# Removing the engine block of a decode kernel and issuing its first loads ahead of the opening barrier

## The chip, the cores and the metric

The kernel runs on one core of one Trainium2 chip. The metric is the measured time of one execution in microseconds (us). The profile of an execution also gives a *span*: from the first to the last instruction record of the program. The two are not the same, the difference between them called the *gap* here (measured time minus span).

## The reference

One decode step of a transformer layer with one token: layernorm, attention over a cache of 32 heads x 4096 positions x 128, and a gated MLP.

```python
x = A_x                                              # [1, 1, 640], bf16
h  = x + attention(layernorm(x), k_cache, v_cache, wq, wo)
h2 = h + (gelu(layernorm(h) @ w_gate) * (layernorm(h) @ w_up)) @ w_down
# k_cache, v_cache: [1, 32, 4096, 128]; wq: [640, 4096]; wo: [4096, 640]; D = 640, Df = 1728
```

The K and V caches are 33.6 MB each, the weights 17 MB: 84.3 MB are read once from HBM for one token.

## The kernel before

The kernel records, per engine, a list of operations with their dependencies, and then emits the lists inside an engine block. A semaphore wait goes in front of each operation that needs one.

```python
    def emit(self, block):
        ...                                   # one semaphore per DMA, one per engine
        for eng in self.ENGINES:
            getattr(block, eng)(lambda e, eng=eng: self._run(e, eng))
```

The first loads are x (issued by ACT) and wq, K group 0, K group 1, V group 0 (issued by SP). Everything later is issued by SP, too, each time a slot of a ring of three comes free.

```python
    d_x = P.dma("scalar", x_row[:, :], A_x[0, :, :])
    ...
    d_wq = [P.dma("sync", arena[:, :], A_wq[:, :].rearrange("(p c) n -> p (c n)", c=5))]
    ...
    issue(NSLOT)                              # K0, K1, V0 into the three slots
```

The end: four copies bring the output row out of PSUM, two on DVE and two on ACT; SP stores it and waits for the store to land.

```python
    os = [V(lambda e, q=q: e.tensor_copy(out_row[0:1, 160 * q:160 * q + 160], ps_d[32 * q:32 * q + 1, 0:160]), dn)
          for q in range(2)]
    os += [A(lambda e, q=q: e.copy(out_row[0:1, 160 * q:160 * q + 160], ps_d[32 * q:32 * q + 1, 0:160]), dn)
           for q in range(2, 4)]
    d_out = P.dma("sync", out[0, :, :], out_row[:, :], *os)
    P.op("sync", None, d_out)                 # SP waits for the store

    with nc.Block() as block:
        P.emit(block)
```

Two things are not in this source. The program object puts an *opening barrier* in front of everything: every engine drains and reports, POOL first fills four constant tiles, and then releases the others. And the block puts a branch in front of each engine's list, a branch after it, and a *closing barrier* of the same kind, with POOL again as the engine that gathers and releases.

The softmax here doesn't subtract the row's maximum and nothing guards it: scores larger than these inputs give would overflow.

## Time and profile before

| | before |
|---|---|
| time, three runs | 205.62, 205.82, 205.85 us |
| span of the profiled run | 204.0 us (its time: 205.85 us) |
| moved by DMA | 84.47 MB, 414 GB/s on average |
| busy share PE / DVE / ACT / POOL | 59% / 49% / 30% / 2% |

From the profile's page of the kernel before: the span in 40 slices of 5.1 us, with the busy share of the 16 DMA engines in tenths (9 is 90% or more) and the rate, then the totals, then the chain that ended last, by engine.

```profile
DMA  7999999999999999999999999999999999999991
GB/s 249 434 442 411 411 488 430 418 411 442 430 430 424 418 427 463 424 419 418 443 450 424 421 424 438 443 430 418 424 434 450 389 440 435 413 409 425 415 393 55
DMA packets 4319, 84.47 MB, mean 414 GB/s; under 512 B 466, under 2 KB 724, under 8 KB 1492
...
DMA 64%; PE 14%; DVE 14%; SPq 4%; issue 3%; DVEq 0%
```

The kernel is a stream of loads with a short head and a short tail. Only the first and last slice are not full. The stretch from 17 to 175 us moves 431 GB/s. The Trainium skill (DMA: Bandwidth & Descriptors, § Specifications) gives a fabric ceiling of 435 GB/s for a core's 16 engines, and this trace agrees with it. (Slices of the page that read higher, such as 488, don't contradict it: the page counts a packet's bytes whole in the slice in which the packet starts. With the bytes spread over each packet's time, no slice of this trace exceeds 434 GB/s.)

The head, from the timeline of the kernel before (start and duration in us, then engine, line, operation, out<-in, count; SPq is SP's queue of DMA issues):

```profile
0.80 0.38 SPq L51 DMA_DIRECT2D arena<-in_A_wq_dram  x1
1.24 0.89 SPq L51 DMA_DIRECT2D slot<-in_A_k_cache_dram  x2
...
2.11 0.35 PE L212 MATMUL bank<-one_bf,x_row 1*128 1x1 bf16 x5 [2.11 <-DMA x_row<-in_A_x_dram]
...
16.35 4.05 PE L238 MATMUL bank<-arena,xlnB 128*32 128x512 bf16 x40 [11.27 <-DMA arena<-in_A_wq_dram]
```

SP issues wq 0.80 us into the span; PE, which needs wq for q, sits idle for 11.27 us until it has landed. What SP did in the first 0.80 us is in its list of waits (who waited for what: us in total, times, longest), kernel before. Of its lines only three matter here:

```profile
SPq L441 <- DMA out_dram<-out_row: 0.8, 1, 0.8
SPq L456 <- PEq L456: 0.7, 1, 0.7
SPq L441 <- PEq L441: 0.2, 1, 0.2
```

L456 is the opening barrier (0.7 us) and L441 the end of the block: the wait for the store, and the closing barrier. (The view names PE as the one that ended the waits at the barriers; by the records further down it is POOL that releases.) The tail, from the timeline of the kernel before:

```profile
201.83 0.60 ACT L436 CAST out_row<-bank 1x160 bf16<-1x160 f32 x2 [5.75 <-PE bank L426]
201.83 0.66 DVE L434 CAST out_row<-bank 1x160 bf16<-1x160 f32 x2 [2.70 <-PE bank L426]
202.52 0.32 SPq L51 DMA_DIRECT2D out_dram<-out_row  x1
```

The timeline leaves out semaphore, branch and drain instructions. The trace has them; these are its last records of the kernel before (start us, duration us, engine, operation):

```
203.668 0.033 SP   COMPARE_BRANCH    waits for the output's semaphore
203.827 0.007 SP   DRAIN             reports to the closing barrier
203.860 0.017 POOL EVENT_SEMAPHORE   all have reported
203.938 0.017 POOL EVENT_SEMAPHORE   releases them
203.980 0.017 SP   EVENT_SEMAPHORE   released (then ACT, DVE)
203.991 0.051 PE   EVENT_SEMAPHORE   released: the last record, span 204.042
```

### The profile page before, as it was taken

How to read it: one execution, taken by the hardware profiler on the slowest of the kernel's cores; microseconds unless marked ns; L12 is line 12 of the kernel's file. 1: busy time of each engine (PE TensorE's matmuls, PEld its weight loads, DVE VectorE, ACT ScalarE, POOL GpSimd, SP SyncE). 2: the span in 40 equal slices, each digit the busy share in tenths (PEclk: the TensorE clock that was granted, in tenths of full speed). 3: DMA queues.
4: the chain of work that ended last, by engine and by line, in shares of the span. 5: the costliest groups of instructions: out<-in, count | busy, mean ns of one | idle time of the engine just before them, and what ended most of it. 6: DMA issues, size and time to landing. Idle time of an engine off the chain costs nothing.

```text
span 204.0 us, 2507 instructions
## 1 busy us (share of the span) xinstructions
PE 121.1 (59%) x1009; PEld 58.9 (29%) x1009; DVE 100.9 (49%) x104; ACT 61.1 (30%) x273; POOL 4.1 (2%) x12
## 2 busy tenths in 40 slices
PE   1007049567667808690977297637834787467494
PEld 1003013122222503250324032312411244267482
DVE  3100187799279327924791677287608760101221
ACT  2100103626706610670156035503630363100101
POOL 8000000000000000000000000000000000000000
PEclk9999757978969975998599859988995899965555
DMA  7999999999999999999999999999999999999991
GB/s 249 434 442 411 411 488 430 418 411 442 430 430 424 418 427 463 424 419 418 443 450 424 421 424 438 443 430 418 424 434 450 389 440 435 413 409 425 415 393 55
DMA packets 4319, 84.47 MB, mean 414 GB/s; under 512 B 466, under 2 KB 724, under 8 KB 1492
## 3 DMA queue, kind: packets, MB, share of 16 engines
q1 hardware_dynamic: 4306, 84.32, 97.0%
q8 instruction: 8, 0.13, 0.3%
q14 instruction: 3, 0.02, 0.0%
q10 hardware_dynamic: 2, 0.00, 0.0%
HBM read 84.31 MB, written 0.00 MB: 413 GB/s over the span
## 4 chain that ended last, share of the span: by engine, by line
DMA 64%; PE 14%; DVE 14%; SPq 4%; issue 3%; DVEq 0%
DMA slot<-in_A_k_cache_dram 43%; DVE prod L252 12%; DMA slot<-in_A_v_cache_dram 11%; DMA slot<-in_B_w_down_dram 10%; PE bank L260 10%; SPq L51 4%; PE bank L289 3%; DVE sc L267 2%; PE bank L298 1%; PE bank L426 0%; DVEq L441 0%; DVE out_row L434 0%; PE bank L309 0%; DVE RT L308 0%
## 5 line engine op out<-in xcount | busy, mean ns | idle before, releaser
L260 PE MATMUL bank<-prod,id_b 128*128 128x512 bf16 x256 | 75.8, 457 | 53.6 <-DVE prod L252 53.5
L252 DVE TENSOR_TENSOR prod<-slot,qb 128x4096 bf16<-128x4096 bf16 x32 | 72.4, 2284 | 31.6 <-DMA slot<-in_A_k_cache_dram 31.6
L271 ACT ACTIVATE p_bd<-sc,zero_t 32x32 bf16<-32x32 f32 x128 | 46.4, 363 | 89.0 <-DVE sc L267 87.8
L260 PEld LDWEIGHTS bank<-prod,id_b 128*128 128x128 bf16 x256 | 27.1, 114 | 102.5 <-DVE prod L252 66.1
L267 DVE TENSOR_REDUCE sc<-bank 128x32 f32<-128x512 f32 x32 | 22.0, 688 | 21.5 <-PE bank L260 21.4
L271 ACT ACTIVATION_READ_ACCUMULATOR p_bd<-sc,zero_t 32x1 f32 x128 | 23.5, 184 | 0.0
L289 PE MATMUL bank<-slot,p_bd 128*16 128x512 bf16 x256 | 17.2, 379 | 0.6 <-DMA slot<-in_A_v_cache_dram 0.6
L289 PEld LDWEIGHTS bank<-slot,p_bd 128*16 128x16 bf16 x256 | 9.4, 89 | 4.8 <-DMA slot<-in_A_v_cache_dram 1.1
L238 PE MATMUL bank<-arena,xlnB 128*32 128x512 bf16 x40 | 4.1, 586 | 11.3 <-DMA arena<-in_A_wq_dram 11.3
L298 PE MATMUL bank<-po_sb,hs 128*16 128x128 f32 x64 | 8.4, 274 | 1.1 <-ACT po_sb L293 1.1
L327 PE MATMUL bank<-aP,arena 128*128 128x1 bf16 x160 | 6.7, 178 | 3.8 <-DMA arena<-in_A_wo_dram 3.8
L396 PE MATMUL bank<-hlnT,slot 128*128 128x1 bf16 (+1 forms) x140 | 6.7, 176 | 3.2 <-DMA slot<-in_B_w_gate_dram 3.2
L327 PEld LDWEIGHTS bank<-aP,arena 128*128 128x128 bf16 x160 | 6.6, 131 | 4.0 <-DMA arena<-in_A_wo_dram 2.6
L396 PEld LDWEIGHTS bank<-hlnT,slot 128*128 128x128 bf16 (+1 forms) x140 | 6.3, 118 | 4.1 <-issue 3.8
L242 DVE CAST qb<-bank 128x512 bf16<-128x512 f32 x1 | 0.7, 692 | 13.8 <-PE bank L238 13.8
L293 ACT COPY po_sb<-bank 128x512 f32<-128x512 f32 x8 | 4.7, 586 | 7.6 <-PE bank L289 7.6
L298 PEld LDWEIGHTS bank<-po_sb,hs 128*16 128x16 f32 x64 | 5.5, 96 | 4.5 <-issue 2.1
L223 ACT ACTIVATE ln<-ln,eps_t 128x1 f32<-128x1 f32 x2 | 0.6, 294 | 17.0 <-DVE ln L221 17.0
L238 PEld LDWEIGHTS bank<-arena,xlnB 128*32 128x32 bf16 x40 | 1.6, 141 | 13.3 <-issue 13.3
L383 DVE TENSOR_TENSOR hT<-xx,bank 128x5 f32<-128x5 f32 x1 | 0.2, 161 | 10.3 <-PE bank L327 10.3
L243 ACT CAST qb<-bank 128x512 bf16<-128x512 f32 x1 | 0.6, 586 | 14.3 <-PE bank L238 14.3
L313 DVE TENSOR_SCALAR aT<-bank,rz 16x128 bf16<-16x128 f32 x2 | 0.7, 339 | 6.0 <-PE bank L298 6.0
(59 smaller groups left out, 24.6 us busy)
## 6 DMA issues: line engine op xcount, KB each, us to landing
slot<-in_A_k_cache_dram SPq DMA_DIRECT2D x8, 4096.0 KB, 22.3
slot<-in_A_v_cache_dram SPq DMA_DIRECT2D x7, 4096.0 KB, 17.4
arena<-in_A_wq_dram SPq DMA_DIRECT2D x1, 5120.0 KB, 15.4
slot<-in_A_v_cache_dram SPq DMA_DIRECT2D x2, 2048.0 KB, 20.9
arena<-in_A_wo_dram SPq DMA_DIRECT2D x1, 2560.0 KB, 28.7
slot<-in_B_w_gate_dram SPq DMA_DIRECT2D x1, 2160.0 KB, 15.4
arena<-in_A_wo_dram SPq DMA_DIRECT2D x1, 1920.0 KB, 32.8
slot<-in_B_w_up_dram SPq DMA_DIRECT2D x1, 1296.0 KB, 18.0
```

Of the source, the lines that this page charges most:

```text
L51: ev = self.op(eng, lambda e: e.dma_start(out, in_), *deps, dma=True)
L238: i = e.matmul(ps_q[hf][32 * j:32 * j + 32, :], xlnB[:, c, :], wq_j[:, c, j, 4 * hf:4 * hf + 4, :], start=(c == 0), stop=(c == 4))
L242: qa = V(lambda e: e.tensor_copy(qb[:, 0:4, :].rearrange("p g d -> p (g d)"), ps_q[0][:, :]), qd)
L252: m = V(lambda e: e.tensor_tensor(out=prod[:, s % 4, :, :], in0=kt[:, 32 * u:32 * u + 32, :], in1=qb[:, G, :].unsqueeze(1).to_broadcast([1 ...
L260: i = e.matmul(ps_f[s % 2][:, :], id_b[:, :], prod[:, s % 4, :, 16 * b:16 * b + 16], start=(b == 0), stop=(b == 7))
L267: reds[s] = V(lambda e: e.reduce_sum(sc[:, s % 4, :], ps_f[s % 2][:, :].rearrange("p (g d) -> p g d", d=16), axis=AX.X), folds[s], exps.ge ...
L271: x = A(lambda e, j=j: e.activation(p_bd[32 * j:32 * j + 32, G % 2, 32 * (s % 4):32 * (s % 4) + 32, j], sc[32 * j:32 * j + 32, s % 4, :], ...
L289: i = e.matmul(po[a:a + 16, :], p_bd[:, G % 2, 4 * b:4 * b + 4, :].rearrange("p g j -> p (g j)"), vt[:, 4 * b:4 * b + 4, :], start=(b < 4) ...
L293: evs[G] = A(lambda e: e.copy(po_sb[:, G % 2, :], po[:, :]), pvs[G], hds.get(G - 2))
L298: i = e.matmul(ps_a[0:16, 128 * (G // 4):128 * (G // 4) + 128], hs[:, r, 12 - 4 * g:28 - 4 * g], po_sb[:, G % 2, 128 * r:128 * r + 128], s ...
L327: r = e.matmul(ps_p[:, c:c + 1], wo_sb[:, t, i, c::5], aP[:, t, i:i + 1], start=(t == 0 and c == 0 and i == 0), stop=(t == 1 and i == 15), ...
L396: i = e.matmul(ps[0 if m < 13 else 64:128, m:m + 1], ws, hlnT[:, c:c + 1], start=(c == 0 and m == 0), stop=(c == 4), skip_group_check=True)
```

## The change

The intent: start the stream earlier by the length of the opening barrier, and drop the block's branches and closing barrier. The loads of x, wq and K0 depend on nothing, so they may be put in front of each engine's drain. The rest of each list follows the barrier in one straight program. The final wait of SP stays.

```diff
-    def emit(self, block):
+    def emit(self, early):
 ...
+        insts = self.nc.cur_bb.bb.instructions
+        for eng, n in early.items():
+            at = next(k for k, i in enumerate(insts) if type(i).__name__ == "InstDrain" and i.engine == getattr(self.nc, eng).engine)
+            old = len(insts)
+            self._run(getattr(self.nc, eng), eng, self.lists[eng][:n])
+            new = insts[old:]
+            del insts[old:]
+            insts[at:at] = new
         for eng in self.ENGINES:
-            getattr(block, eng)(lambda e, eng=eng: self._run(e, eng))
+            self._run(getattr(self.nc, eng), eng, self.lists[eng][early.get(eng, 0):])
 ...
-    with nc.Block() as block:
-        P.emit(block)
+    P.emit({"sync": 2, "scalar": 1})
```

More of the change, by code (lines that the diff above doesn't have):

```diff
@@ L69, in emit, with _run @@
                     ev.sem, ev.count = sem, n
+        insts = self.nc.cur_bb.bb.instructions
[6 more added lines that the diff above has]
+            insts[at:at] = new
         for eng in self.ENGINES:
-            getattr(block, eng)(lambda e, eng=eng: self._run(e, eng))
-    def _run(self, e, eng):
+            self._run(getattr(self.nc, eng), eng, self.lists[eng][early.get(eng, 0):])
+    def _run(self, e, eng, ops):
         seen = {}
-        for fn, deps, ev in self.lists[eng]:
+        for fn, deps, ev in ops:
             need = {}
```

## The prediction

> **What bounds the kernel now.** HBM traffic. The page's DMA line shows 84.47 MB at a mean of 414 GB/s in a span of 204.0 us, and a busy share of 9 tenths in every slice but the first (7) and last (1). Counting the trace's packets, all 16 DMA engines are in use without a gap from 1.81 us, where wq's first packet starts, to about 200 us; the last weight packet ends at 200.81. The compute engines are far below (page: PE 59%, DVE 49%, ACT 30%). The chain of waits is 64% DMA. So the time is a head, a saturated stream of 199 us, and a tail (down matmuls, output store, closing barrier).
>
> **What the change does.** No arithmetic, byte, transfer size or order within an engine changes. Each engine loses two branches, all lose the closing barrier, and three DMA issues (x on ACT, wq and K group 0 on SP) move ahead of the opening barrier.
>
> 1. Head (timeline): SP reaches the opening barrier at 0.00 us, is released at 0.72, after POOL's four constant memsets, branches, and issues wq at 0.80 (0.38 us), K0 at 1.24 (0.42), K1 at 1.71. The first packet starts 1.01 us after the issue. Issued at 0.00, it starts at about 1.0: **-0.80 us**, all on the critical path, because the stream behind it never starves. The barrier now waits for SP's two issues and opens at about 1.0 us, so the other engines' setup starts 0.2 to 0.3 us later. That has slack: layernorm ends at 6.7 us and PE waits until 16.35 for wq (11.3 us idle). K1 is issued at about 1.1, with 9 MB still queued.
>
> 2. Branch: the 0.07 us from SP's release to the wq issue includes it, inside the 0.80. The Trainium skill (Runtime: NRT & Kernel Launch, § Instruction fetch mechanics) says that a taken branch outside the fetched pages stalls for a fetch; this trace shows no such stall here. Eight instruction pages of 16 KB (about 1 us each on one DMA engine) are fetched along the way and remain: 0.
>
> 3. Tail: the output's packets end at 203.33 us, SP's wait record is at 203.67, then a branch, a drain at 203.83, and the barrier releases the last engine by 204.04. Without them the program ends with SP's wait, at about 203.70: **-0.34 us**. The same page (§ The ~15µs preamble/postamble breakdown) says the runtime has its own barrier after the kernel, so this one is redundant; no record here shows that. The 1.8 us between span and measured time (205.85) I take as fixed.
>
> Sum: -1.14 us, 0.6%.
>
> **Predicted time: 204.7 us, 204.2 to 205.4 in 8 of 10.** Faster by over 2%: 0.01; within 2%: 0.98; slower by over 2%: 0.01.
>
> **What would show it.** SP's wq issue is the span's first record and wq's first packet starts about 1.0 us into it; wq matmuls start at about 15.5 us; all later landings are about 0.8 us earlier; bytes and busy times unchanged; the last record is SP's wait, about 0.35 us after the output's packet; span about 202.9 us. Wrong if the first packet is not earlier, or if the head's gain shrinks along the stream.
>
> **What would make it wrong.** The measured time may start at something that the early issues don't precede, or end at the runtime's barrier, which absorbs the tail's 0.34: then 204.9 to 205.5. SP's drain might wait for its transfers: the barrier would open some 20 us late and everything slip; improbable. The throttle's half-speed windows (granted clock 0.5 in the tail) may shift against the down matmuls, +-0.2 us.

## The result, and the profile after

| | before | after |
|---|---|---|
| time, median of six runs | 205.62 us (205.38 to 205.85) | 204.24 us (203.40 to 204.52) |
| ratio | | 0.9925, 95% interval 0.9905 to 0.9945 |
| span of the profiled run | 204.04 us | 202.90 us |
| its time | 205.85 us | 204.16 us |
| its gap | 1.8 us | 1.3 us |

Ratios are the mean time of one kernel's fast runs over that of the other's fast runs of the same rounds, so they are not quite the ratio of the medians quoted. The ratio times 205.62 us is 204.08 us.

The change saved 1.4 to 1.7 us, about 0.75%, so the two kernels are the same within 2%, as forecast. The span of this pair fell by the predicted 1.14 us; that it fits to the hundredth is luck, since the spans of the six runs of the changed kernel run from 202.1 to 203.3 us. But the time of the profiled run fell by 1.69 us. The rest lies outside the span, where the profile shows nothing.

The page of the changed kernel, the same parts as of before:

```profile
DMA  9999999999999999999999999999999999999992
GB/s 356 412 422 452 420 413 426 446 455 428 368 426 439 426 423 452 420 428 439 426 439 433 430 426 415 452 439 426 420 430 420 417 436 426 426 407 434 411 401 87
DMA packets 4319, 84.47 MB, mean 416 GB/s; under 512 B 466, under 2 KB 724, under 8 KB 1492
...
DMA 65%; PE 15%; DVE 15%; issue 3%; SPq 2%
```

The same packets and bytes; of the busy shares only those of the first and the last slice changed, and the first slice went from 249 to 356 GB/s. The head, from the timeline of the changed kernel:

```profile
0.00 0.39 SPq L51 DMA_DIRECT2D arena<-in_A_wq_dram  x1
...
0.44 1.15 SPq L51 DMA_DIRECT2D slot<-in_A_k_cache_dram  x2
...
5.40 0.35 PE L221 MATMUL bank<-one_bf,x_row 1*128 1x1 bf16 x5 [5.40 <-DMA x_row<-in_A_x_dram]
...
15.28 4.46 PE L247 MATMUL bank<-arena,xlnB 128*32 128x512 bf16 x40 [8.47 <-DMA arena<-in_A_wq_dram]
```

SP now issues wq as the first record of the span. In the packets of the trace, the first one starts at 1.004 us (before: 1.813) and the last weight packet ends at 200.11 us (before: 200.81). The x row came 3.3 us later than before in this trace (5.40 against 2.11 us), its packet starting at 3.45 us. That is not a property of the change: in the repeat of the same kernel (after_same, below) the packet starts at 1.005 us and PE takes x at 1.53 us, earlier than before. Why it was late here, no run shows. PE still waits 8.47 us for wq afterwards, so it costs nothing.

The waits of SP in the changed kernel; L464 is the opening barrier, L93 the waits of the program:

```profile
SPq L93 <- DMA out_dram<-out_row: 0.8, 1, 0.8
SPq L464 <- PEq L464: 0.2, 1, 0.2
```

SP's wait at the opening barrier went from 0.7 to 0.2 us, and the one at a closing barrier is gone. The tail in the timeline of the changed kernel:

```profile
201.05 0.60 ACT L445 CAST out_row<-bank 1x160 bf16<-1x160 f32 x2 [5.76 <-PE bank L435]
201.05 0.66 DVE L443 CAST out_row<-bank 1x160 bf16<-1x160 f32 x2 [2.73 <-PE bank L435]
201.73 0.31 SPq L51 DMA_DIRECT2D out_dram<-out_row  x1
```

and the trace's last record:

```
202.884 0.017 SP   EVENT_SEMAPHORE   waits for the output's semaphore: the last record, span 202.901
```

In the changed kernel no other engine has a record after 201.71 us, and POOL has none after 5.3 us.

### The profile page after: what moved, and what is told of

It reads as the page before. It is cut to its first block, busy times and chain, and to the rows that moved or that the text cites. A ratio compares the mean times of both kernels' runs of the same rounds, so it can differ in the third digit from the quotient of the medians.

```text
span 202.9 us, 2496 instructions
## 1 busy us (share of the span) xinstructions
PE 122.3 (60%) x1009; PEld 59.2 (29%) x1009; DVE 100.9 (50%) x104; ACT 61.1 (30%) x273; POOL 4.1 (2%) x12
## 4 chain that ended last, share of the span: by engine, by line
DMA 65%; PE 15%; DVE 15%; issue 3%; SPq 2%
DMA slot<-in_A_k_cache_dram 43%; DVE prod L261 12%; DMA slot<-in_B_w_down_dram 11%; DMA slot<-in_A_v_cache_dram 11%; PE bank L269 10%; PE bank L298 3%; DVE sc L276 2%; SPq L51 2%; PE bank L307 1%; PE bank L435 1%; DVE out_row L443 0%; PE bank L318 0%; DVE RT L317 0%
## 5 line engine op out<-in xcount | busy, mean ns | idle before, releaser
L269 PE MATMUL bank<-prod,id_b 128*128 128x512 bf16 x256 | 76.7, 461 | 52.7 <-DVE prod L261 52.6
```

The lines of the kernel that those rows point to most:

```text
L269: i = e.matmul(ps_f[s % 2][:, :], id_b[:, :], prod[:, s % 4, :, 16 * b:16 * b + 16], start=(b == 0), stop=(b == 7))
```

## The experiments

The question: why did the measured time fall by 0.4 to 0.55 us more than the span? Theory T says that it is the end. In the kernel before, all engines leave the program together, held by the closing barrier. In the changed kernel the others leave early and do their part of what the runtime does after the kernel while SP still waits for the store. Rival H says that it is the head (the measured time starts at something that moved closer to the span). Rival B says that it is the branches of the block.

Four kernels ran on one chip, with 11 runs of the kernel before beside them (median 205.51 us; mean time 205.54, mean span 203.78, mean gap 1.75). The gap is the quantity to watch: spans scatter by some 0.5 us from run to run, gaps by less than 0.1 us around their mean. (Spans are on record to 0.1 us, so the gap of a single run is good to 0.05 us.)

### block_early: the early issues alone, with block and closing barrier

```diff
         for eng in self.ENGINES:
-            self._run(getattr(self.nc, eng), eng, self.lists[eng][early.get(eng, 0):])
+        with self.nc.Block() as block:
+            for eng in self.ENGINES:
+                getattr(block, eng)(lambda e, eng=eng: self._run(e, eng, self.lists[eng][early.get(eng, 0):]))
```

> The early issues alone: the engine block with its branches and its closing barrier stays. 'Gap' is the measured time minus the span (1.85 us in the profiled run of before, 1.26 in that of after). All theories: wq is the first record, the first packet is about 1.0 us into the span, the span is about 0.80 us under that of before (203.2). Theory T (the additional 0.55 us comes from the end: without a closing barrier the engines other than SP go on into what the runtime does after the kernel while SP still waits for the output): gap stays 1.85, time about 0.8 us under before. Theory H (it comes from the head: the measured time starts at something that early issues let come closer to the span): gap 1.3, time about 1.35 us under before.

Measured: correct; median 204.94 us, ratio 0.9982 (0.9963 to 1.0001); mean gap 1.78 (1.72 to 1.84). The gap stays at the value of before, as theory T has it and H has not. The first packet starts at 1.006 us, as in the changed kernel. The mean span is 203.35, only 0.43 us under that of before (median 203.15, 0.65 under); this is taken up again below.

### straight_late: the straight program alone, without early issues

```diff
-    P.emit({"sync": 2, "scalar": 1})
+    P.emit({})
```

> The straight program without the early issues: branches and closing barrier are gone, x, wq and K0 are issued after the opening barrier as before. All theories: first packet at about 1.8 us, span about 0.35 us under before (203.7). Theory T: gap 1.3, time about 0.9 us under before. Theory H: gap 1.85, time about 0.35 us under before.

Measured: correct; median 204.83 us, ratio 0.9964 (0.9947 to 0.9981); mean span 203.47 (0.32 us under before), mean gap 1.305 (1.22 to 1.40). The first packet is at 1.80 us, as before, and still the gap has fallen by 0.45 us. Theory T holds and H falls: the gap belongs to how the program ends, not to how it starts.

### straight_barrier: the changed kernel with a barrier at its end

```diff
     P.emit({"sync": 2, "scalar": 1})
+    nc.all_engine_barrier()
```

> The changed kernel with an all-engine barrier at its end, without block and branches. Span about 203.1 (0.15 to 0.3 us over that of the changed kernel). Theory T: gap back to 1.85, time about 0.8 us under before. Theory B (the branches, and the fetch of what follows them, are what costs, not the barrier): gap 1.3, time about 1.4 us under before. Theory H: gap 1.3, too, but then block_early has 1.3 as well.

Measured: correct; median 204.72 us, ratio 0.9964 (0.9947 to 0.9982); mean span 202.97, mean gap 1.805 (1.73 to 1.87). A barrier without block and branches brings the gap back: rival B falls. In the traces, SP's drain starts 0.056 us after the start of its wait for the store here and 0.159 us after it in block_early, so the branch costs about 0.10 us at the end; that cost is inside the span.

### straight_allwait: all engines wait for the store, no barrier

```diff
-    P.op("sync", None, d_out)
+    for eng in ("sync", "gpsimd", "vector", "tensor", "scalar"):
+        P.op(eng, None, d_out)
```

> The changed kernel in which all five engines, not SP alone, wait for the output's semaphore; no drain, no barrier, no branch. Span as that of the changed kernel, or 0.05 us more. Theory T (it is the late arrival of the other engines at the runtime's part that costs): gap about 1.8, time about 1.0 us under before. If the barrier's own instructions cost it, or theory H: gap 1.3, time about 1.5 us under before.

Measured: correct; median 204.59 us, ratio 0.9957 (0.9941 to 0.9974); mean span 202.72, mean gap 1.807 (1.77 to 1.85). There is no barrier, drain or branch at the end, and the gap is 1.8 again. It is the late arrival of other engines that costs, whatever makes them late.

### wait_tensor, wait_vector, wait_scalar, wait_gpsimd: one engine waits, not SP

The next question was whether one engine in particular is expensive to hold, or the joint arrival. Another chip; 7 runs of before beside them (mean span 203.74, mean gap 1.75). The edit, with the engine's name changed in each:

```diff
-    P.op("sync", None, d_out)
+    P.op("gpsimd", None, d_out)
```

> The changed kernel, with PE instead of SP as the one engine that waits for the output. The gap (measured time minus span) is the quantity; the span should be as that of the changed kernel (202.8) within its scatter of some 0.5 us. Theory L (each engine has its own length of work between its last instruction and the end of the measured time; the last arrival sets it, and SP's is short): at least one of the four engines tried shows 1.8, the others something of their own. Theory N (no engine's own length matters; the gap is 1.8 when several engines arrive together with SP and 1.3 when one comes last alone): 1.3 for all four. For PE, theory L: 1.8 (it has the longest program).

> The same with DVE as the one that waits. Theory L: between 1.3 and 1.8, its own value. Theory N: 1.3.

> The same with ACT as the one that waits. Theory L: between 1.3 and 1.8, its own value. Theory N: 1.3.

> The same with POOL as the one that waits. Theory L: between 1.3 and 1.8, its own value. Theory N: 1.3.

All four are correct. Four runs of each, and for SP the two times six runs of the changed kernel:

| the engine that ends last | median time | ratio | mean span | mean gap (range) |
|---|---|---|---|---|
| DVE | 203.77 | 0.9913 | 202.40 | 1.39 (1.34 to 1.41) |
| ACT | 203.56 | 0.9907 | 202.20 | 1.47 (1.40 to 1.52) |
| PE | 204.18 | 0.9924 | 202.58 | 1.55 (1.48 to 1.59) |
| POOL | 204.49 | 0.9946 | 202.60 | 1.85 (1.81 to 1.92) |
| SP (the changed kernel, other chips) | 204.24, 204.06 | 0.9925, 0.9921 | 202.78, 202.62 | 1.30 (1.22 to 1.40) |

In each of the four traces the waiting engine has the last record, 0.85 us or more after SP's last, so the edit did what it should. The gaps differ by engine, so theory L holds and N falls; PE's expected 1.8 was a miss, POOL has it. POOL stands clear of the rest. The steps between SP, DVE, ACT and PE are about 0.1 us each and their ranges touch, so their order is less certain. (The lower times of DVE and ACT come from their spans, not from their gaps, and SP did not run on that chip; the gap of before is 1.75 on it, as on the others.)

POOL's value explains the gaps of the other kernels that end with all engines, to within 0.04 us, if the measured time ends at the latest of *an engine's last record + its own length*. POOL's last record ends at 203.955 us in the kernel before: 203.955 + 1.853 - 204.042 = 1.77 (measured 1.75). The same sum gives 1.77 for block_early (1.78), 1.77 for straight_barrier (1.81) and 1.82 for straight_allwait (1.81). In all four it is POOL that the end waits for by this sum; the same sum for PE, the next in length, gives 1.55.

### after_same, block_early2, straight_late2: whole and halves on one chip

block_early had saved less span than its first packet promised. So the whole change and both halves ran once more, together, with 11 runs of before (mean time 205.57, mean span 203.83, mean gap 1.745). The edits are those above; after_same has none.

> The changed kernel without an edit, on the same chip as its two halves and with spans of all its runs and of those of before. Span 1.0 to 1.15 us under before, gap 1.30 against 1.75, together 1.45 to 1.6 us under before. If the parts add, it is the sum of the two runs after it.

> A repeat of the early issues alone, because the first measurement of it (0.4 us under before, span 0.43 under) was less than the 0.80 that its first packet promises. If the 0.80 us carries through to the end (theory S: the stream only moves, and its scatter of some 0.3 us from run to run hid it), the mean span is 0.7 to 0.9 us under that of before. If the stream gives part of it back in a program with the block (theory G), it is again 0.4 to 0.5. Gap 1.75 in both.

> A repeat of the straight program with late issues, to add to the run above: span 0.35 us under before, gap 1.30, together 0.8 us under before.

| | median time | ratio | mean span (less than before) | mean gap |
|---|---|---|---|---|
| after_same | 204.06 | 0.9921 (0.9904 to 0.9938) | 202.62 (1.21) | 1.30 |
| block_early2 | 205.06 | 0.9983 (0.9967 to 1.0) | 203.40 (0.43) | 1.77 |
| straight_late2 | 204.71 | 0.9965 (0.9942 to 0.9988) | 203.53 (0.29) | 1.29 |

The whole comes out a little over what was expected: 1.21 us of span (1.0 to 1.15 expected) and 0.44 us of gap, 1.65 us together (1.45 to 1.6 expected). The gaps of the halves are as expected, too. The spans of the halves add to 0.72 us in the means, against 1.21; in the medians they come nearer (before 203.9, early issues alone 203.3, straight alone 203.35, both 202.8: 0.6 and 0.55 against 1.1). For block_early both measurements gave 0.43, which is what theory G named (0.4 to 0.5) and not theory S (0.7 to 0.9); the standard error of the two together is about 0.12 us, an estimate from the scatter of the runs. Its kept traces don't show where it would be lost. In them the stream from the first to the last weight packet took 199.03 and 199.11 us, against 199.00 in the trace of before and 199.10 in that of after, and the last weight packet ended at 200.04 and 200.14 us, 0.7 to 0.8 us ahead of before. Single traces can't show it, either: over the fourteen kept traces, all with the same loads, the stream took 198.2 to 199.9 us. straight_barrier, with early issues and a barrier at its end but no block, had a mean span 0.81 us under before; less the 0.10 us of the branch, some 0.7 us of this is the head's, an estimate. So the shortfall shows only with the block. Whether the early issues lose some of their gain when the block is kept, or the scatter of the stream is still in the way after twelve runs, stays open. The changed kernel has no block.

### after_onecast: one copy per engine at the end

The trace's tail suggested a further gain: each of DVE and ACT makes two copies of one partition, one after the other (0.31 us each).

```diff
-    out_row = sb("out_row", [1, D], BF16)
+    out_row = sb("out_row", [128, 160], BF16)
 ...
-    os = [V(lambda e, q=q: e.tensor_copy(...), dn) for q in range(2)]
-    os += [A(lambda e, q=q: e.copy(...), dn) for q in range(2, 4)]
-    d_out = P.dma("sync", out[0, :, :], out_row[:, :], *os)
+    os = [V(lambda e: e.tensor_copy(out_row[0:33, :], ps_d[0:33, 0:160]), dn),
+          A(lambda e: e.copy(out_row[64:97, :], ps_d[64:97, 0:160]), dn)]
+    d_out = P.dma("sync", out[0, :, :].rearrange("o (q n) -> (o q) n", q=4), out_row[0:97:32, :], *os)
```

> The changed kernel with the output's four copies out of PSUM made by one instruction on each of DVE and ACT (33 partitions each) in place of two. The second copy of each engine, 0.31 us in the trace, is on the tail's chain: span and time 0.31 us under the changed kernel, if the output's store from four partitions lands as fast as from one (1.15 us from issue to SP's wait). Gap 1.30.

Measured, on the same chip: correct; median 204.46 us, ratio to before 0.9945 (0.9929 to 0.9961), mean span 203.10, which is 0.48 us over after_same. A miss. Its tail in the timeline:

```profile
200.48 0.29 ACT L444 CAST out_row<-bank 33x160 bf16<-33x160 f32 x1 [5.87 <-PE bank L435]
200.48 0.32 DVE L443 CAST out_row<-bank 33x160 bf16<-33x160 f32 x1 [2.86 <-PE bank L435]
200.86 0.63 SPq L51 DMA_DIRECT2D out_dram<-out_row  x1
```

The copies did take 0.3 us less: the store is issued 0.38 us after their start (200.86 - 200.48), against 0.68 in the changed kernel (201.73 - 201.05). But the issue of a store from four partitions took 0.63 us in place of 0.31, and from its start to SP's wait went 1.66 us (200.86 to 202.51) in place of 1.15. The store lost 0.51 us and the copies won 0.31, a loss of 0.2 us by the records; the means of the runs say 0.48, with the stream's scatter in them. No version tried beats the changed kernel clearly.

## Why the prediction was right or wrong

- **Bound by the stream: right.** The bytes and packets did not change, the stream took 199.0 us before and 199.1 after, and in the changed kernel what moved its start moved the end.
- **Head, -0.80 us: right for the changed kernel.** The first packet starts 0.81 us earlier (1.004 against 1.813), the last weight packet 0.71 us earlier in the profiled pair. The wq matmuls start at 15.28 us (about 15.5 predicted). SP's drain did not wait for its transfers. The barrier opened at 1.18 us and not at 1.0, for the most part because SP's drain took 0.125 us (0.007 before); without effect, like the late x of the profiled run. The early issues with the block kept gave only 0.43 us, which the prediction's account does not explain.
- **Branch, 0 at the head: right.** From SP's release to the wq issue it is 0.07 us with the branch (before) and without it (straight_late).
- **Tail inside the span, -0.34 us: right.** SP's wait starts 0.350 us after the output's packet (0.345 before), and the span is 202.9 us as predicted. Without early issues the straight program took 0.32 and 0.29 us off the mean span. The traces split the gain: about 0.10 for the branch, the rest for the barrier.
- **The step that failed: "The 1.8 us between span and measured time (205.85) I take as fixed."** It is not fixed. It is 1.75 us on average with the closing barrier and 1.30 us without it, and this term of -0.44 us was missing from the sum: -1.14 - 0.44 = -1.58 us, against -1.38 (medians), -1.54 (ratio) and -1.65 (repeat) measured. So the time came to 204.1 to 204.2 us where 204.7 was forecast, at and below the low end of the range. A further 0.2 us of the miss lies in the base: 204.7 is 205.85 less 1.14, and 205.85 was the slowest of the six runs of before, whose median is 205.62.
- **Behind it, a wrong idea of what a redundant barrier costs.** The prediction read in the Trainium skill (Runtime: NRT & Kernel Launch, § The ~15µs preamble/postamble breakdown) that the runtime has a barrier of its own after the kernel, and took from it only that the closing one is superfluous. As a risk it even named the opposite sign, that the runtime's part would absorb the tail's 0.34 us. The runs show that the engines have work of different lengths between their last instruction and the end of the measured time (SP 1.30, DVE 1.39, ACT 1.47, PE 1.55, POOL 1.85 us), and that a closing barrier lets the longest of them, POOL's, start only when the output has landed. What that work is, no record here shows.

## What to carry to other kernels

When a kernel is one saturated stream of loads, its first issue belongs ahead of the opening barrier: the barrier's 0.8 us came off the span of the whole change, within the scatter (with the block kept, only 0.43 did). Leave no barrier at the end and let the engine with the shortest way out (here SP, though against DVE and ACT the measured times don't decide) be the only one that waits for the output; holding POOL to the end costs 0.55 us more, and the profile doesn't show it. So compare the measured time with the span in every run: their difference is a term of the sum like any other.

## What the Trainium skill lacked or had wrong

- Runtime: NRT & Kernel Launch, § The ~15µs preamble/postamble breakdown, gives the work after the kernel as stages with one time each. It lacks that the time from an engine's last instruction to the end of the measured time differs by engine. Its three stages after the kernel add up to about 5 us, an estimate from its figures, and the whole gap is less than 2 us, so they can't all lie in the gap at those times. The gap was 1.30 us with SP last, 1.39 with DVE, 1.47 with ACT, 1.55 with PE and 1.85 with POOL.
- DMA: Bandwidth & Descriptors, § Specifications, gives about 0.6 us to the first byte of a DMA issued by SP or ACT, and doesn't say from where it counts. For wq the first packet starts 0.62 us after the end of the issue (1.004 - 0.388) and 1.00 us after its start, which is what an earlier issue moves. For small transfers it varied: from the end of the issue 0.39 us for x in the kernel before, 2.81 us for x in the profiled run of the changed kernel, and 0.43 us for its output.
- No page that was read gives the price of spreading a tiny store over partitions: 1280 bytes from four partitions took 0.51 us longer from the start of the issue to SP's wait record than from one (1.66 against 1.15 us).
